# Weight conversions placed anew in a fused attention and two-MoE kernel: later ones apart, earlier ones at one step

## The chip, the cores and the metric

The kernel runs on one core of a Trainium2 chip. The metric is the device time in microseconds of one execution. Times below are of the kernel on its own, with all data in the chip's memory at the start.

## The reference

Three layers follow one another, all in float32 (the weights come in as float64 words and are used at a precision above one float32r product):

```python
kv  = einsum('bhsd,bhse->bhde', k, v)          # 8 batches, 8 heads, 576 tokens, 64 wide
x   = einsum('bhsd,bhde->bhse', q, kv)
x   = x / sqrt(mean(x*x, -1) + 1e-6) * g_norm  # then reshaped to 4608 tokens x 512
h   = x @ w_in;  x = relu(h)**2 @ w_out        # 512 -> 2048 -> 512, weights A
h   = x @ w_in;  out = (h * cos(h)) @ w_out    # 512 -> 2048 -> 512, weights B
```

## The kernel before

Every matrix product is made of three float32r products of a high and a low half (high x high, high x low, low x high), so each operand is split: ScalarE (ACT) casts the high half and VectorE (DVE) subtracts it to get the low one.

**Stage one** (`run_chunks`, L842) makes the attention, and with it one half of the first MoE layer (eight of the sixteen 128-wide slices of its hidden dimension). Its unit is a chunk: one tile of 512 tokens and one slice `f`. There are nine tiles; the last two (7 and 8) have 4 chunks each and the others 8, so `nA0` = 64 chunks. A chunk makes 12 matmuls into a bank (`layer_in`, L409), has relu and square (`act_relu2`), and two chunks later (`LAG`) 12 more (`layer_out`, L443). At a tile's last chunk `evict` (L424) copies the four accumulators out, the even ones on ACT, the odd ones on DVE, and stores each two of them to `p_d`. Up to chunk 49 (`nAtt`) the attention of later batches runs between the chunks.

**Stage two** (`run_slots`, L870) makes the rest by a scheme of seven products in place of eight for each 2x2 block product (Strassen's, in Winograd's form). A slot is one pair of token half-tiles and one group of hidden slices, with 84 first-product matmuls (L532, banks FA and FB) and the second products (L665, banks SA and SB) that follow 1.25 slots later (`LAG2`). There are 31 slots: 0 to 10 for the rest of the first MoE layer, 11 to 30 for the second. Slots 0 to 3 and 8 to 22 have matmuls of 512 columns, 4 to 7 and 23 to 30 of 384. In a slot DVE makes sums of hidden blocks, low halves (L642), differences (L618) and drains of the S banks (L693); ACT makes relu or the cosine's parts and the high halves (L641). Blocks of the inputs (`x_block`, L487 to L506) of a tile are made from about 0.64 slot before the tile's first slot to 0.5 after its start.

**The weight conversions** give stage two its weights: a raw block is loaded from memory, turned from float64 words to float32 (L121 to L135: four DVE steps, one ACT step, then one more DVE step), combined into seven blocks (four subtractions or additions, L199), split (cast L216 on ACT, L218 on DVE), and stored to `wi_d` (first weights) or `ws_d` (second), from where each slot loads them (L511, L516). `conv_steps` (L186) is a generator; its steps are placed at offsets 0, 0.25, 0.5, 0.75, 1.0, 1.25 chunks from the item's place in stage one and at 0, 0.07, 0.15, 0.22, 0.3, 0.4 slots in stage two (`Stream.place`, L728). The kinds of items:

- "seven" and "pair" (stage one): a half of a pair of slices, 512 elements a partition, for the second and the first weights; the load of the item after next is issued 1.4 chunks after an item's place, into the same two buffers.
- "pairs" (stage two): a whole pair, 1024 elements a partition, from float64: the heavy kind.
- "pairs32" and "sevens32" (stage two): a whole pair that stage one has already turned to float32 and stored in `wf_d`, so that only L199, L216 and L218 are left: the light kind.

The late stream has one raw buffer. An item's load is issued `lead` = 0.5 slot ahead of its place, but no earlier than 0.62 slot after the place of the item before.

What sets the order of the work is written by hand: all jobs have a position in chunks or slots, `run_jobs` emits them in that order between the matmuls, and the tile framework assigns buffers and semaphores and has some freedom in the order on an engine. All loads and stores of the parts named here are issued by the sync engine (SP), in order; POOL issues the attention's stores and the accumulating adds of the second MoE layer.

Of the kernel before, what the change touches and what calls it, by code (L numbers as in the profile page):

```python
# [22 lines left out]
def kernel(  # L23
# [15 lines left out]
    nc = tc.nc  # L39
# [3 lines left out]
    NH = NF // 2  # L43
    NP = NH // 2
# [14 lines left out]
    FS = [NH // 2 if any(TILES[u][0] <= t * TOK < TILES[u][0] + 2 * TILES[u][1] for u in SHORT) else NH for t in range(NTILE)]  # L59
# [364 lines left out]
    def evict(t, i, acc):  # L424
        if i % 2 == 0:
            evs[t, i // 2] = ev_p.tile([P, 2, 512], F32, tag="ev", name="ev")
        both = evs[t, i // 2]
        if i % 2 == 0:
            nc.scalar.copy(out=both[:, 0, :], in_=acc)
        else:  # L430
            nc.vector.tensor_copy(out=both[:, 1, :], in_=acc)  # L431
            nc.sync.dma_start(out=p_d[t][:, i - 1:i + 1, :], in_=both)

    def layer_out(t, f):
        wh, wl = (x[:, 1, :] for x in wts[0, f])
        gh, gl = gs.pop((t, f))
        for i in range(NKC):
            if f == 0:
                accs[i] = bank_tile(f"acc{i}")
            o = accs[i]  # L440
            cs = slice(i * P, (i + 1) * P)
            for n, (a, m) in enumerate(((wh, gh), (wh, gl), (wl, gh))):
                nc.tensor.matmul(  # L443
                    o, a[:, cs], m[:], start=(f == 0 and n == 0), stop=(f == FS[t] - 1 and n == 2), skip_group_check=True
                )
            if f == FS[t] - 1:
                evict(t, i, o)
# [258 lines left out]
    nA0 = len(chunks)  # L706
    nAtt = 49
# [6 lines left out]
    def pos(slot):  # L714
        return nA0 + slot + 0.002
# [27 lines left out]
    def pairs_in(m, ps, kind="pair"):  # L743
        return [(kind, m, p, i) for p in ps for i in range(2)]
# [5 lines left out]
        w_at += [n + step * k for k in range(len(new))]  # L750
    for new, n0, n1 in (
        (
            pairs_in(0, range(NP, 2 * NP), "seven") + pairs_in(1, range(2 * NP), "seven"),
            10,
            nAtt + 1,
        ),
        (pairs_in(0, range(NP, 2 * NP)), nAtt + 1, nA0 - 5),
    ):
        w_items += new
        w_at += [n0 + (n1 - n0) / len(new) * k for k in range(len(new))]  # L760
    w_stream = Stream(load_w, conv_w, w_items)
    w_stream.place(w_at, 0.5, range(2 * NH - NRAW, 2 * NH - NRAW + 2))
    late_stream = Stream(load_w, conv_w, (
        [("pairs", 1, p, 0) for p in range(NP)]
        + [(kind, 0, p, 0) for kind in ("pairs32", "sevens32") for p in range(NP // 2, NP)]
        + [("pairs", 1, p, 0) for p in range(NP, 2 * NP)]
    ))
    late_stream.place([pos(n) for n in (0.55, 1.25, 2.5, 3.2, 4.5, 5.2, 6.5, 7.2, 8.5, 9.3, 11.5, 12.3)], 0, lead=0.5)

    kv_stream = Stream(load_kv, kv_mm, [(b, c) for b in range(B) for c in range(NSC)])  # L770
    starts = [(-13, 1), (-3, 0.8)] + [(-3 + 7 * (b - 1), 7 / (2 * NKC)) for b in range(2, B)]
# [3 lines left out]
    for b, (s0, ds) in enumerate(starts):  # L775
        for i, u in enumerate(att_units(b)):
            n = s0 + i * ds
# [21 lines left out]
    for k, (m, t, q) in enumerate(slots):  # L799
# [7 lines left out]
        for f, i in enumerate(S_ORDER):  # L807
            at(pos(k + LAG2 + (f - 2.7) * PH), load_ws, k, i)
            n = LAG2 + (f - 1.6) * PH
# [14 lines left out]
        for b, f in BLOCKS.items():  # L824
            for a, fn in enumerate(chain):
                late = 0.3 if f == 7 and a > 1 else 0
                n = (f + late + 0.25 * (a + 1)) * PH
# [159 lines left out]
```

## Time and profile before

| | |
|---|---|
| median of 3 runs | 1575.92 us (1573.0 to 1578.34) |
| profiled execution | 1575.98 us, span 1574.1 us |
| granted TensorE clock, mean | 0.995 |
| PE busy | 98% of the span |
| DVE, ACT, POOL busy | 83%, 70%, 7% |
| DMA | 445.58 MB, mean 283 GB/s |
| stage one | 0 to 457 us |
| slots 0 to 10 | 457 to 874 us (with the last second products running on) |
| slots 11 to 30 | from about 874 us to the end |

The span runs from the first to the last instruction; 1.9 us of the execution lie outside it. PE is TensorE with its matmuls, PEld its weight loads, and a window's clock is the granted share of full speed: 1.00 is 2.4 GHz and 0.50 is 1.2 GHz, the engine's two levels. A row of waits names the engine that stood, the line of the instruction that stood, the instruction whose end released it, the sum, the count and the longest. SPq is SP's queue of DMA issues.

### The profile page before, as it was taken

Reading aid. Unit: us, or ns where it says so; the run is one execution under the profiler, and the core shown is the slowest. Engines: PE = TensorE matmul, PEld = TensorE weight load, DVE = VectorE, ACT = ScalarE, POOL = GpSimd, SP = SyncE. Lnnn points to the kernel's source line nnn. Section 1 sums busy time; section 2 is a strip of 40 time slices with the busy share of each in tenths; the row PEclk is TensorE's granted clock in tenths of the full one; section 3 lists DMA queues with packets and bytes.
Section 4 is the critical chain, followed back from the end, with each engine's and each line's share of the span. In section 5 each row is a group of like instructions: output and inputs, shape, how many; then the busy total and the mean of one; then the engine's idle time right before and its main releaser. Section 6 shows DMA issues by size and latency. Waiting matters only on the chain.

```text
span 1574.1 us, 24732 instructions
## 1 busy us (share of the span) xinstructions
PE 1535.6 (98%) x9080; PEld 1344.6 (85%) x9080; DVE 1309.8 (83%) x1747; ACT 1102.3 (70%) x1554; POOL 114.5 (7%) x181
## 2 busy tenths in 40 slices
PE   6899999999998999999999999999999999999998
PEld 4677777778787878998888899999999999999998
DVE  6987888887788999979889978967896788779777
ACT  6877777775566565656657777777777777777775
POOL 1122111110000000000000000000000000000001
PEclk9999999999999999999999999999999999999999
DMA  9858989777898898999997798787888788999896
GB/s 337 282 180 243 281 268 282 223 212 227 280 329 311 296 353 298 402 400 356 347 374 232 274 322 250 238 293 221 255 235 293 215 247 264 292 323 306 275 336 168
DMA packets 232072, 445.58 MB, mean 283 GB/s; under 512 B 19728, under 2 KB 144144, under 8 KB 231952
## 3 DMA queue, kind: packets, MB, share of 16 engines
q1 hardware_dynamic: 219536, 406.91, 74.7%
q0 software_dynamic: 12256, 37.10, 10.8%
q8 instruction: 72, 1.18, 0.3%
q14 instruction: 48, 0.39, 0.1%
q10 hardware_dynamic: 160, 0.00, 0.0%
HBM read 327.16 MB, written 91.23 MB: 266 GB/s over the span
## 4 chain that ended last, share of the span: by engine, by line
PE 74%; DMA 10%; DVE 9%; issue 3%; ACT 3%; SPq 0%; POOL 0%; DVEq 0%; ACTq 0%; POOLq 0%
PE SA L665 15%; PE SB L665 14%; PE FB L532 14%; PE FA L532 14%; PE acc L443 7%; PE l L409 6%; DMA wi_d<-raw 2%; DMA wi<-wi_d 1%; DMA raw<-in_wA 1%; DMA ws_d<-raw 1%; DMA raw<-in_wB 1%; DVE gl L642 1%; DVE sum L693 1%; DVE raw L218 1%; DMA xraw<-x_d 1%
## 5 line engine op out<-in xcount | busy, mean ns | idle before, releaser
L532 PE MATMUL FA<-xh,wi 128*128 128x512 f32 (+1 forms) x872 | 313.0, 371 | 1.0 <-ACT h L571 0.6
L532 PE MATMUL FB<-xh,wi 128*128 128x512 f32 (+1 forms) x864 | 311.7, 372 | 0.1
L665 PE MATMUL SA<-ws,gh 128*128 128x256 f32 x1008 | 232.9, 280 | 0.2 <-ACT part L690 0.2
L665 PE MATMUL SB<-ws,gh 128*128 128x256 f32 x1008 | 232.5, 280 | 0.0
L665 PEld LDWEIGHTS SB<-ws,gh 128*128 128x128 f32 x1008 | 183.3, 188 | 12.0
L665 PEld LDWEIGHTS SA<-ws,gh 128*128 128x128 f32 x1008 | 183.2, 188 | 12.1 <-ACT part L690 0.4
L532 PEld LDWEIGHTS FA<-xh,wi 128*128 128x128 f32 x872 | 163.5, 188 | 13.3 <-ACT h L571 1.0
L532 PEld LDWEIGHTS FB<-xh,wi 128*128 128x128 f32 x864 | 162.5, 189 | 11.5 <-ACT u L552 0.5
L665 PE MATMUL SA<-ws,gl 128*128 128x256 f32 x504 | 141.3, 280 | 0.3 <-DVE gl L642 0.3
L665 PE MATMUL SB<-ws,gl 128*128 128x256 f32 x504 | 141.3, 280 | 0.1
L642 DVE TENSOR_TENSOR gl<-y,gh 128x1024 fp32r<-128x1024 f32 (+1 forms) x98 | 109.5, 1117 | 35.7 <-ACT gh L641 35.5
L691 POOL DMA_DIRECT2D sum<-part x54 | 47.2, 874 | 1149.3 <-ACT part L690 561.6
L602 DVE SCALAR_TENSOR_TENSOR y<-y,h 128x1024 f32<-128x1024 f32 (+1 forms) x79 | 88.2, 1116 | 43.0 <-ACT y L598 42.8
L665 PE MATMUL SA<-gh,ws 128*128 128x512 f32 (+1 forms) x312 | 114.5, 379 | 6.6 <-ACT wh L216 4.2
L584 ACT ACTIVATE y<-h,zerob 128x1024 int32<-128x1024 f32 (+1 forms) x79 | 84.1, 1065 | 48.2 <-DVE h L558 48.1
L532 PE MATMUL FA<-xl,wi 128*128 128x512 f32 (+1 forms) x312 | 115.9, 371 | 0.0
L532 PE MATMUL FB<-xl,wi 128*128 128x512 f32 (+1 forms) x308 | 114.6, 372 | 0.0
L665 PE MATMUL SB<-gh,ws 128*128 128x512 f32 (+1 forms) x304 | 108.4, 370 | 0.0
L443 PE MATMUL acc<-gh,wh 128*128 128x512 f32 x256 | 100.6, 398 | 4.2 <-DVE ev L431 1.7
L693 DVE TENSOR_TENSOR sum<-SA,sum 128x1024 f32<-128x1024 f32 (+1 forms) x78 | 87.4, 1121 | 19.2 <-PE SA L665 14.9
L594 ACT ACTIVATE y<-y 128x1024 f32<-128x1024 f32 (+1 forms) x79 | 77.2, 977 | 34.7 <-DVE y L588 34.6
L443 PE MATMUL acc<-gl,wh 128*128 128x512 f32 x256 | 100.6, 393 | 0.3 <-DVE gl L421 0.3
(172 smaller groups left out, 3840.4 us busy)
## 6 DMA issues: line engine op xcount, KB each, us to landing
wi<-wi_d SPq DMA_DIRECT2D x217, 512.0 KB, 6.9
ws<-ws_d SPq DMA_DIRECT2D x217, 512.0 KB, 6.2
sum<-part POOLq DMA_DIRECT2D x33, 512.0 KB, 7.2
kvld<-in_kv SPq DMA_DIRECT2D x32, 512.0 KB, 7.6
ws_d<-raw SPq DMA_DIRECT2D x24, 448.0 KB, 4.5
q<-in_qT SPq DMA_DIRECT2D x32, 288.0 KB, 5.3
p_d<-ev SPq DMA_DIRECT2D x18, 512.0 KB, 4.9
wi_d<-raw SPq DMA_DIRECT2D x10, 896.0 KB, 7.1
```

The source lines that it names most:

```text
L218: nc.vector.tensor_tensor(out=l[:, lo:end], in0=a[:, lo:end], in1=as32(h), op=ALU.subtract)
L409: nc.tensor.matmul(ps, a[:, 0, cs], m[:], start=(c == 0 and k == 0), stop=(c == NKC - 1 and k == 2))
L443: nc.tensor.matmul(o, a[:, cs], m[:], start=(f == 0 and n == 0), stop=(f == FS[t] - 1 and n == 2), skip_group_check=True)
L532: nc.tensor.matmul(ps[:, pp, :], a, b, start=(n == 0 and (i in (0, 2) or i == 1 and not seeded(k))), stop=(n == 5), skip_group_check=True,)
L584: nc.scalar.activation(out=y.bitcast(I32), in_=hs[k, b], func=AF.Identity, bias=zerob)
L594: nc.scalar.activation(out=y, in_=y, func=AF.Sin, scale=math.pi)
L602: nc.vector.scalar_tensor_tensor(out=y, in0=y, scalar=-2.0 * math.pi, in1=hs.pop((k, b)), op0=ALU.add, op1=ALU.mult)
L642: nc.vector.tensor_tensor(out=l, in0=src, in1=as32(h), op=ALU.subtract)
L665: nc.tensor.matmul(ps[:, b, :], lhs, rhs, start=(n == 0 and (m == 0 or b % 2 == 0) and i in (0, 1, 2)), stop=(n == 5), skip_group_check=True,)
L691: nc.gpsimd.dma_start(out=e, in_=part, accum_op=ALU.add)
L693: nc.vector.tensor_tensor(out=e, in0=ps, in1=e, op=ALU.add)
```

## The change

Three edits. In `evict` the odd accumulators of the two short tiles (7 and 8) are copied by ACT too. In stage one, the conversions from chunk 10 on stand at one step up to `nA0 - 3` = 61: 34 items, 1.5 chunks apart, where 24 stood 1.667 apart from 10 to 50 and then 8 stood 1.125 apart to 59; their order mixes "seven" and "pair" items, and the two halves of pair 0 of the second layer's first weights are new among them. In stage two that pair is gone from the late list, which has 11 items at other places: pairs 1 (0.95), 2 (2.5), 3 (4.5), 4 (6.5), 5 (9.2), 6 (10.2), 7 (11.4) of the second layer are heavy, with the four light ones at 3.4, 5.4, 7.4 and 8.3. Before, heavy ones stood at 0.55, 1.25, 2.5, 3.2, 8.5, 9.3, 11.5 and 12.3 and the light ones at 4.5, 5.2, 6.5 and 7.2.

```diff
         both = evs[t, i // 2]
-        if i % 2 == 0:
-            nc.scalar.copy(out=both[:, 0, :], in_=acc)
+        if i % 2 == 0 or FS[t] < NH:
+            nc.scalar.copy(out=both[:, i % 2, :], in_=acc)
         else:
             nc.vector.tensor_copy(out=both[:, 1, :], in_=acc)
+        if i % 2:
             nc.sync.dma_start(out=p_d[t][:, i - 1:i + 1, :], in_=both)
...
     for new, n0, n1 in (
         (
-            pairs_in(0, range(NP, 2 * NP), "seven") + pairs_in(1, range(2 * NP), "seven"),
+            pairs_in(0, range(NP, 2 * NP), "seven")
+            + pairs_in(1, range(2), "seven")
+            + pairs_in(0, range(NP, NP + 2))
+            + pairs_in(1, range(2, 2 * NP), "seven")
+            + pairs_in(0, range(NP + 2, 2 * NP))
+            + pairs_in(1, range(1)),
             10,
-            nAtt + 1,
+            nA0 - 3,
         ),
-        (pairs_in(0, range(NP, 2 * NP)), nAtt + 1, nA0 - 5),
     ):
...
-    late_stream = Stream(load_w, conv_w, (
-        [("pairs", 1, p, 0) for p in range(NP)]
-        + [(kind, 0, p, 0) for kind in ("pairs32", "sevens32") for p in range(NP // 2, NP)]
-        + [("pairs", 1, p, 0) for p in range(NP, 2 * NP)]
-    ))
-    late_stream.place([pos(n) for n in (0.55, 1.25, 2.5, 3.2, 4.5, 5.2, 6.5, 7.2, 8.5, 9.3, 11.5, 12.3)], 0, lead=0.5)
+    late_stream = Stream(load_w, conv_w, [
+        ("pairs", 1, 1, 0), ("pairs", 1, 2, 0), ("pairs32", 0, 2, 0), ("pairs", 1, 3, 0), ("pairs32", 0, 3, 0),
+        ("pairs", 1, 4, 0), ("sevens32", 0, 2, 0), ("sevens32", 0, 3, 0),
+        ("pairs", 1, 5, 0), ("pairs", 1, 6, 0), ("pairs", 1, 7, 0),
+    ])
+    late_stream.place([pos(n) for n in (0.95, 2.5, 3.4, 4.5, 5.4, 6.5, 7.4, 8.3, 9.2, 10.2, 11.4)], 0, lead=0.5)
```

## Rows read from the trace of the kernel before

**Rows 1.** The page's busy time, share of the span and instructions.

```profile
PE 1535.6 (98%) x9080; PEld 1344.6 (85%) x9080; DVE 1309.8 (83%) x1747; ACT 1102.3 (70%) x1554; POOL 114.5 (7%) x181
```

**Rows 2.** Windows by stage: length, each engine's busy time, granted clock, DMA share, GB/s.

```profile
100.00:350.00 250.00, 248.69 (x1546) 194.08 (x1545) 206.07 (x471) 193.76 (x429) 46.16 (x86) 1.00 0.82 249
...
405.00:450.00 45.00, 41.91 (x182) 33.40 (x181) 35.85 (x65) 27.66 (x45) 0.00 (x0) 1.00 0.96 321
...
517.00:595.00 78.00, 76.88 (x338) 62.84 (x337) 73.37 (x74) 47.52 (x50) 0.00 (x0) 1.00 0.92 326
595.00:662.00 67.00, 67.00 (x348) 61.70 (x346) 60.62 (x67) 41.49 (x51) 0.00 (x0) 1.00 0.91 339
662.00:727.00 65.00, 61.18 (x336) 60.07 (x336) 52.64 (x62) 36.24 (x46) 0.00 (x0) 0.95 1.05 402
727.00:836.00 109.00, 108.90 (x501) 92.29 (x500) 95.05 (x97) 64.17 (x68) 0.00 (x0) 1.00 0.92 341
836.00:874.00 38.00, 38.00 (x169) 31.50 (x168) 37.08 (x37) 25.80 (x26) 0.00 (x0) 1.00 0.77 253
```

**Rows 3.** PE's waits in the whole span: us in total, times, longest.

```profile
PE SA L665 <- ACT wh L216: 4.2, 1, 4.2
PE SA L665 <- ACT gh L641: 2.3, 1, 2.3
...
PE acc L443 <- DVE ev L431: 1.7, 1, 1.7
```

**Rows 4.** Windows around the two largest waits of PE, columns as in rows 2.

```profile
492.00:498.00 6.00, 1.76 (x8) 1.21 (x7) 6.00 (x7) 2.58 (x4) 0.00 (x0) 0.86 0.80 326
498.00:504.00 6.00, 6.00 (x17) 4.66 (x17) 6.00 (x8) 4.03 (x5) 0.00 (x0) 0.57 0.93 329
704.00:711.00 7.00, 3.32 (x14) 2.49 (x13) 6.66 (x10) 3.71 (x5) 0.00 (x0) 0.78 1.05 401
711.00:716.00 5.00, 5.00 (x20) 5.00 (x20) 4.61 (x5) 2.82 (x4) 0.00 (x0) 0.62 1.05 413
```

**Rows 5.** Timeline at the first stall: start, duration, engine, line; idle before in brackets.

```profile
488.29 0.69 DVE L121 TENSOR_SCALAR e<-raw 128x1024 uint32<-128x1024 uint32 x1 [1.03 <-DMA raw<-in_wB]
...
495.18 1.22 DVE L135 SCALAR_TENSOR_TENSOR raw<-w,e 128x1024 f32<-128x1024 uint32 x1
496.32 1.22 DVE L693 TENSOR_TENSOR sum<-SA,sum 128x1024 f32<-128x1024 f32 x1
496.44 0.83 ACT L216 CAST wh<-raw 128x768 fp32r<-128x768 f32 x1 [3.42 <-DVE raw L135]
...
497.64 0.77 PE L665 MATMUL SA<-gh,ws 128*128 128x512 f32 x1 [4.24 <-ACT wh L216]
```

**Rows 6.** Timeline ahead of the second stall, ACT.

```profile
700.62 0.84 ACT L216 CAST wh<-raw 128x768 fp32r<-128x768 f32 x1 [5.40 <-DMA raw<-wf_d]
```

**Rows 7.** DVE's waits from 405 to 450 us.

```profile
DVE e L121 <- DMA raw<-in_wA: 7.2, 2, 3.9
```

**Rows 8.** SP's longest wait in 100:350; DMA issues: KB each, median us to landing.

```profile
SPq L145 <- DMA ws_d<-raw: 57.3, 21, 4.9
...
ws_d<-raw SPq DMA_DIRECT2D x24, 448.0 KB, 4.5
...
raw<-in_wA SPq DMA_DIRECT2D x24, 256.0 KB, 3.8
```

**Rows 9.** Conversion steps in slots 0 to 11, shapes apart: busy us, mean ns.

```profile
L199 DVE TENSOR_TENSOR raw<-raw 128x256 f32<-128x256 f32 x48 | 18.4, 420 | 0.3
L218 DVE TENSOR_TENSOR raw<-raw,wh 128x1024 fp32r<-128x1024 f32 x12 | 14.6, 1218 | 0.3 <-ACT wh L216 0.3
...
L126 DVE SCALAR_TENSOR_TENSOR w<-raw,w 128x1024 uint32<-128x1024 uint32 x8 | 9.7, 1217 | 0.0
```

**Rows 10.** Groups by line: copies of the accumulators on DVE and ACT.

```profile
L431 DVE COPY ev<-acc 128x512 f32<-128x512 f32 x18 | 12.3, 686 | 4.8 <-PE acc L443 4.8
...
L429 ACT COPY ev<-acc 128x512 f32<-128x512 f32 x18 | 10.3, 593 | 4.8 <-PE acc L443 4.8
```

## The prediction, made before the change was run

> **What bounds the kernel now.** I began with the busy shares of the page [rows 1]: TensorE is busy in 1535.6 of the 1574.1 us of the span, so about 38.5 us of idle time, and whatever it ran at half clock, is all that a change of order can win. The windows come next [rows 2], cut where the stages and slots end (a slot is 84 first-product matmuls, so its borders are counted from the matmuls). PE is idle 1.3 us in the attention part (100 to 350 us), 3.1 us at the end of stage one (405 to 450), 1.1 us in slots 2 and 3, nothing in 595 to 662, 3.8 us in 662 to 727, and next to nothing after. The rest lies ahead of 100 us, at the end, and in slot 1, and the change does not touch the first two.
>
> The waits of PE [rows 3] name the places: 4.2 us for the cast `wh` of a weight conversion, 2.3 us for a cast `gh`, 1.7 us for DVE's copy of an accumulator. Cut finer, both large waits show a second cost [rows 4]. From 492 to 498 PE was busy 1.76 of 6 us, so 4.24 idle; then for 6 us it was busy throughout at a granted clock of 0.57, which is mostly the 1.2 GHz level. That loses 6 x 0.43 = 2.6 us more, and with 0.2 at the edge the first stall cost **7.0 us**. The second: 7 - 3.32 = 3.7 us idle, 5 x 0.38 = 1.9 us in the row after it, and about 0.7 in matmuls at half clock before 711: **6.3 us**.
>
> Why the first happened stands in its timeline [rows 5]. The conversion of pair 1 (second in the late list, at 1.25) reached DVE at 488.29; its last step L135 ran at 495.18, and only behind it came the sum that empties bank SA, at 496.32. It ended at 497.5, and PE's next SA matmul began at 497.64. ACT's cast waited for the same L135. So DVE's queue was full, and the conversion stood ahead of a drain. The second has another cause [rows 6]: ACT stood 5.40 us at a cast because the raw weights of a light item had not landed, and everything behind it on ACT was late, the relu chain and `gh` among it. In the old list that item follows the one before by 0.7 slot, and its load is only issued 0.62 after that one's start, 0.08 slot ahead of its use: 2.4 us at 29 us a slot.
>
> **The change, part by part.** All sums are against the profiled execution, 1575.98 us, which is 0.06 above the median shown.
>
> *End of stage one.* Eight conversions stood 1.125 chunks apart there, which with a reload 1.4 chunks behind the use of two items earlier leaves 0.85 chunk, 4.6 us at 5.44 us a chunk. DVE waited 7.2 us, in two waits, for raw weights [rows 7], and the copy L431 behind them held PE for 1.7 [rows 3]. At 1.5 chunks the lead is 1.6 chunks, 8.7 us. A store and a load need about 4.5 + 3.8 us [rows 8], so most of it goes. The last two tiles' second and fourth copies (4 instructions, 0.69 us on DVE, 0.59 on ACT) [rows 10] leave that queue too; ACT has room (27.7 of 45 us), so I cost them at nothing; if ACT is late, a bank comes free 0.6 us late. Of 3.1 us idle I take **-2.6** (bounds -3.1 and 0). Two more conversions, halves of pair 0, stand at 58 and 59.5, and they take buffers of the block pool while the blocks of slot 0 are made; a late store there holds ACT, which the two chunks of lag (10.9 us) cover. The two halves issue 8 DMAs on SP where the whole issued 5, of equal bytes, beside loads not wanted before slot 0.
>
> *Attention part.* The step goes from 1.667 to 1.5 chunks, so some 26 items stand where there were 23. One costs DVE near 5 us (about 0.6 of a heavy late one, below), so 206 of 250 us busy becomes 219 [rows 2], and PE has 1.3 us idle to show for the present load. The reload lead falls from 1.93 to 1.6 chunks, 10.7 us at 6.7 us a chunk. SP already waits 57.3 us there, 21 times, for a store to land before a reload [rows 8]. Cover: that lead and the two chunks of lag. Bounds 0 and +8 (rival C). I take **+1.0**, near the present idle time. The Trainium skill ("DMA: Bandwidth & Descriptors", "Anatomy of one DMA") puts most of a DMA's fixed cost, about 2 us, into the receipt of its write, with a fit of 2.0 us plus bytes over 436 GB/s; worked out from the page, an estimate, store and load would take 5.7 us and this term would be 0. The trace has 8.3 us for the pair, and the measurement decides.
>
> *Slots 0 and 1.* Pair 0 is gone from 0.55 and pair 1 moves from 1.25 to 0.95, so DVE has one heavy item fewer and the other off its drains. A heavy item costs DVE 2 x 0.69 (L121, L123) + 3 x 1.22 (L126, L132, L135) + 4 x 0.38 (L199) + 1.22 and about 0.95 for its piece of three quarters (L218) = 8.7 us; a light one lacks the first five, and costs 3.7 [rows 5, 9]. The stall goes: **-7.0**. In its place: the item now stands just ahead of the first operand of the second products, wanted at 1.25, 0.3 slot or 5.7 us after it. One L121, an ACT step of about 1.1, two 1.22s, then the casts and the rest of that operand (0.8 + 1.0 + 1.2) come to 7.4 us, 1.7 late. I take **+2.0**; it is 0 if DVE starts early, and 5 if the wait costs half clock as the second stall did.
>
> *Slots 2 and 3.* One heavy item becomes light; the 1.1 us idle goes: **-0.8** (0 to -1.1).
>
> *Slot 7.* The item now has 0.28 slot, 8 us, from load to use in place of 2.4. The raw weights landed 5.40 us after ACT wanted them, so 5.7 us more lead just covers it. The stall goes: **-6.3** (0 if DMA, at 1.05 of its share there [rows 2], takes longer).
>
> *Slots 4 to 7, DVE.* Two light items become heavy (4.5 and 6.5), +2 x 5.0 us. DVE was busy 60.6 + 52.6 of 132 us, idle 18.8 [rows 2], with 6 of that in the stall. It fits on the sum, to 123 of about 126, but locally it is full. A drain may be late by one block of 12 matmul pairs (4.2 us at 384 columns) before PE feels it. Bounds: 0, and all 10; I take **+2.0**.
>
> *Slots 8 to 12.* The heavy item at 12.3 moves to 10.2, ahead of slot 11, whose window (836 to 874) has DVE busy 37.1 of 38 us while PE loses nothing; 727 to 836 has 14 us of room [rows 2]. Bounds 0 and 8; **+1.0**.
>
> Sum: -2.6 + 1.0 - 7.0 + 2.0 - 0.8 - 6.3 + 2.0 + 1.0 = -10.7, so 1575.98 - 10.7 = **1565.3 us**. With the best bounds all round it is -17.5, 1558.5.
>
> **Rivals.**
> A: the new waits (2 + 2 + 1 + 1 = 6 us) each drop the clock. Both stalls shown cost about 1.7 times their idle time [rows 4], so +4.2: 1569.5. Against it: the wait of 1.7 us at 418 left the clock at 1.00 in its window [rows 2, 3]. The Trainium skill ("TensorE: Matmul & The Clock Gate", "HAM oscillation") says that repeated waits re-throttle the engine and the return is paid each time; the trace agrees for the two large waits, not for the short one. By that rule this rival is the forecast.
> B: the stalls only move. The 0.95 item delays the first second product by as much as the 1.25 item did the drain, and DVE in slots 4 to 7 makes one stall of 6.3 us: -2.6 + 1.0 - 0.8 - 6.3 + 6.3 + 1.0 = -1.4, 1574.6. For it: the scheduler orders DVE's queue by its own idea of time, and moved no drain ahead of L135 [rows 5].
> C: reloads late in the attention part, five times, at what each of the two waits in rows 7 cost PE (3.1 / 2 = 1.55): +8 for +1, 1572.3. Against: 3.8 + 4.5 us is below the lead.
> D, slower: DVE becomes the bound from slot 4 on, and its idle time can't be used, as it is waiting for ACT and PE. Then all added DVE time is paid: +10 in slots 4 to 7 and +8 before slot 12 instead of +3, and each stretch drops the clock once, 2 x 2.6 more: -10.7 + 15 + 5.2 = +9.5, 1585.5. It turns the sign when over 13.7 of these 23.2 us are paid, and can be told from no change from 18.4 on. For it: slot 11 is already full. Against it: 595 to 662 ran DVE at 60.6 of 67 with no PE idle, so lateness is absorbed.
>
> **How the numbers follow.** About 0.3% (4.7 us) is what a measurement of this kernel can tell from no change, so faster means below 1571.2 and slower above 1580.6. Forecast 0.54, A 0.12: both faster, 0.66. B 0.17 and C 0.05: the same, 0.22. D: 0.12. The likeliest case alone spans 1558.5 (all new waits nil) to 1571. Leaving out D's upper part and a little at the bottom, the range is 1558 to 1577, which takes in A, B and C.
>
> **What would show it.** Right: no PE wait over 2 us between 457 and 914, the granted clock 1.00 in every 25 us there, no wait of DVE for raw weights behind chunk 50, PE idle near 1 us in 100 to 350. Wrong: a PE wait at the first second product with the clock at half behind it (B), PE waiting for drains around 4.5 to 5 or 6.5 to 7 or at slot 11 with DVE busy 99% (D), or many DVE waits for raw weights in the attention part (C). The forecast fails above all if DVE at 98% in slots 4 to 7 leaves PE no slack.

## The result and the profile after

The changed kernel takes **1584.59 us** (median of 5 runs, 1582.74 to 1585.82) against 1574.78 us for the kernel before in the same series: ratio **1.0058, interval [1.0043, 1.0074]**. It is slower by 0.6%, where the prediction had 1565.3 and 1558 to 1577. The profiled execution has a span of 1583.8 us, at a mean granted clock of 0.993.

Counted from the matmuls, slot 0 starts at 476.8 us, before at 457.2: stage one lost **19.6 us**. From the start of slot 0 to the start of slot 12 it is 406.6 us against 416.6: those slots won **10.0 us**. The other 19 slots moved by under 1 us. (By the same count slots 0 to 10 of the kernel before end at 836 us and slot 11 at 874; where the table of before and two of the expectations say slots 0 to 10, they mean 0 to 11.)

The busy row of the page, to be held against [rows 1], shows next to no change:

```profile
PE 1536.8 (97%) x9080; PEld 1345.3 (85%) x9080; DVE 1307.6 (83%) x1755; ACT 1103.2 (70%) x1562; POOL 114.0 (7%) x181
```

The windows by stage have the columns of [rows 2]; in the order of the rows: the attention part, the largest stall in it and the stretch behind, the end of stage one (moved by the 19 us), slots 0 and 1, 2 and 3, 4 to 7, 8 to 11.

```profile
100.00:350.00 250.00, 235.49 (x1457) 182.04 (x1456) 200.11 (x462) 181.98 (x404) 41.40 (x79) 0.97 0.82 248
175.00:182.00 7.00, 1.34 (x7) 0.81 (x5) 2.60 (x6) 0.73 (x2) 0.00 (x0) 0.73 0.96 243
182.00:188.00 6.00, 6.00 (x25) 4.33 (x26) 4.58 (x13) 3.57 (x8) 2.11 (x4) 0.74 0.73 195
424.00:469.00 45.00, 42.04 (x174) 34.23 (x173) 33.98 (x58) 25.82 (x41) 0.00 (x0) 0.92 0.97 316
476.00:530.00 54.00, 54.00 (x240) 44.72 (x239) 44.90 (x43) 38.56 (x41) 0.00 (x0) 1.00 0.92 322
530.00:606.00 76.00, 76.00 (x338) 62.94 (x337) 69.44 (x70) 46.21 (x49) 0.00 (x0) 1.00 0.89 309
606.00:735.00 129.00, 124.86 (x678) 118.79 (x677) 118.47 (x135) 76.87 (x95) 0.00 (x0) 1.00 0.97 357
735.00:885.00 150.00, 149.06 (x675) 124.59 (x674) 136.94 (x139) 93.27 (x97) 0.00 (x0) 1.00 0.92 340
```

PE is idle 14.5 us in 100 to 350, where it was 1.3 [rows 2], and DVE is *less* busy there, 200 against 206 us, although the change asks it for more: fewer items passed in that time. At the end of stage one the idle time is as large as before (3.0 against 3.1), now with the clock down to 0.92 behind it. In slots 0 to 3 it is nil.

PE's longest waits by now, whole span (columns as in [rows 3]; the last line is from before); both `SA` waits of before are gone:

```profile
PE ss L346 <- DVE m L359: 12.7, 6, 5.7
PE o L285 <- DMA kvld<-in_kv: 11.0, 5, 8.6
PE l L409 <- ACT r L418: 3.1, 4, 1.1
PE acc L444 <- ACT ev L429: 3.0, 1, 3.0
...
PE ss L346 <- DVE m L359: 1.3, 2, 0.7
```

The second row lies ahead of 100 us and is as before. The first is new in size, 12.7 us against 1.3: the attention's norm has a single bank, `ss`, which DVE's step L359 empties. What DVE waits for in 100 to 350 says why it is late: 19.1 us in 9 waits for raw weights, where the same view of before (the last two lines) adds up to 5.4 in 3.

```profile
DVE e L121 <- DMA raw<-in_wA: 11.7, 5, 5.6
...
DVE e L121 <- DMA raw<-in_wB: 7.4, 4, 2.8
...
DVE e L121 <- DMA raw<-in_wB: 3.9, 2, 3.5
...
DVE e L121 <- DMA raw<-in_wA: 1.5, 1, 1.5
```

One stall in full, from the timelines of SP, DVE and PE (start, duration, engine, line):

```profile
165.56 0.68 SPq L221 DMA_DIRECT2D ws_d<-raw  x1
166.34 2.51 SPq L273 DMA_DIRECT2D kvld<-in_kv  x2
173.03 1.28 SPq L145 DMA_DIRECT2D raw<-in_wA  x3
...
179.36 0.43 DVE L121 TENSOR_SCALAR e<-raw 128x512 uint32<-128x512 uint32 x1 [5.63 <-DMA raw<-in_wA]
181.37 0.45 DVE L359 SCALAR_TENSOR_TENSOR m<-ss,r 128x288 f32<-128x288 f32 x1
...
181.87 0.61 PE L346 MATMUL ss<-sh,ones 128*128 128x288 f32 x1 [5.66 <-DVE m L359]
```

A conversion's last store is issued at 165.56, among the loads of keys and values. SP then stands until it has landed, since the reload goes into the same buffer, and issues the reload at 173.03. DVE gets at it at 179.36 and had waited 5.63 us; the norm's step L359 stands behind it in DVE's queue, and PE behind that. From 175 to 188 us the granted clock is also down, to 0.73 and 0.74 in the two windows above.

### The profile page after: what moved, and what is told of

Read it like the earlier page. It is cut to its first block, busy times and chain, and to the rows that moved or that the text cites. A ratio compares the mean times of both kernels' runs of the same rounds, so it can differ in the third digit from the quotient of the medians.

```text
span 1583.8 us, 24760 instructions
## 1 busy us (share of the span) xinstructions
PE 1536.8 (97%) x9080; PEld 1345.3 (85%) x9080; DVE 1307.6 (83%) x1755; ACT 1103.2 (70%) x1562; POOL 114.0 (7%) x181
## 3 DMA queue, kind: packets, MB, share of 16 engines
q0 software_dynamic: 12256, 37.10, 10.7%
## 4 chain that ended last, share of the span: by engine, by line
PE 70%; DMA 13%; DVE 6%; issue 6%; ACT 4%; SPq 1%; POOL 0%; DVEq 0%; POOLq 0%; ACTq 0%
PE FB L533 14%; PE FA L533 14%; PE SA L666 14%; PE SB L666 14%; PE acc L444 6%; PE l L409 5%; DMA ws_d<-raw 3%; DMA sum<-part 2%; DMA ws<-ws_d 2%; DMA raw<-in_wA 1%; DMA wi_d<-raw 1%; DVE raw L218 1%; DVE gl L643 1%; DMA kvld<-in_kv 1%; DVE sum L694 1%
## 5 line engine op out<-in xcount | busy, mean ns | idle before, releaser
L666 PEld LDWEIGHTS SA<-ws,gh 128*128 128x128 f32 x1008 | 183.2, 188 | 12.5 <-ACT part L691 0.7
L533 PEld LDWEIGHTS FA<-xh,wi 128*128 128x128 f32 x872 | 163.2, 188 | 10.7
L666 PE MATMUL SA<-gh,ws 128*128 128x512 f32 (+1 forms) x312 | 110.5, 371 | 0.5 <-issue 0.3
L444 PE MATMUL acc<-gh,wl 128*128 128x512 f32 x256 | 102.0, 398 | 0.0
```

The source lines that it names most:

```text
L444: nc.tensor.matmul(o, a[:, cs], m[:], start=(f == 0 and n == 0), stop=(f == FS[t] - 1 and n == 2), skip_group_check=True)
L533: nc.tensor.matmul(ps[:, pp, :], a, b, start=(n == 0 and (i in (0, 2) or i == 1 and not seeded(k))), stop=(n == 5), skip_group_check=True,)
L666: nc.tensor.matmul(ps[:, b, :], lhs, rhs, start=(n == 0 and (m == 0 or b % 2 == 0) and i in (0, 1, 2)), stop=(n == 5), skip_group_check=True,)
```

## The experiments

Five theories stand against each other, and the expectations use these letters. **T**: the reload is placed too late. **L**: DVE has too much work. **S**: SP, an in-order queue, stands for a store to land, and other transfers are late behind it. **E**: the DMA engines are full in the bursts of five loads of keys and values (one batch's, issued together every 7 chunks). **K**: the cycle of the two raw buffers is too slow for the step of 1.5 chunks; three of the expectations have it under an earlier name, T2. (O, in two of them, blames the new order of the items.) "Before" and "after" are the two kernels of the case, and each ratio is to before in the run's own series.

### Which part of the change wins and which loses

Late places alone, on the kernel before:

```diff
-        [("pairs", 1, p, 0) for p in range(NP)]
...
+        ("pairs", 1, 1, 0), ("pairs", 1, 2, 0), ("pairs32", 0, 2, 0), ("pairs", 1, 3, 0), ("pairs32", 0, 3, 0),
+        ("pairs", 1, 0, 0), ("sevens32", 0, 2, 0), ("sevens32", 0, 3, 0),
...
+    late_stream.place([pos(n) for n in (0.95, 2.5, 3.4, 4.5, 5.4, 6.5, 7.4, 8.3, 9.2, 10.2, 11.4, 12.3)], 0, lead=0.5)
```

> The late list alone: the kernel before, with the new places for the late conversions and pair 0 kept among them (at 6.5, so the heavy ones after it move one place on and the last stands at 12.3). If the two parts are independent (stage one lost about 19 us, the slots won about 9), stage one ends as before, slot 0 begins at 457 us, slots 0 to 10 take 408 to 411 us in place of 417.5, and the time is 1565 to 1569 us. If the slots won only because pair 0 had left them, slots 0 to 10 take 415 to 420 and the time is 1572 to 1578.

Measured 1569.14 us, 0.9962 [0.9951, 0.9974]; slots 0 to 11 take 406.7 us. The other way round, after's stage one with the old late places (without pair 0):

> Stage one and the copies as changed, the late conversions at their old places (without pair 0). If the parts are independent, slot 0 begins at 475 to 478 us, the stall in slot 7 (6.3 us) comes back and the one in slot 1 partly; slots 0 to 10 take 410 to 417 us and the time is 1586 to 1594 us. If the loss in stage one came with the late list, slot 0 begins at 457 to 460.

1589.27 us, 1.0092 [1.0076, 1.0109]. The late part wins about 6 us alone and the rest loses about 14; together that is the loss of the whole change to within 1 us. In slots 0 to 11 the two overlap: they take 408.9 us without pair 0 at the old places, 406.7 with it at the new ones, and 406.6 with both edits. Slot 0 starts at 478.6 us in this run, so the fault lies in stage one.

There the change has three parts: a new order, a new step, and copies on ACT. The new order at the old step up to chunk 50, and the rest behind it:

```diff
-            nA0 - 3,
-        ),
...
+    w_at += [10 + (nAtt - 9) / 24 * k for k in range(24)] + [nAtt + 1 + (nA0 - nAtt - 4) / 10 * k for k in range(10)]
```

> The changed kernel with the old step of 1.667 chunks up to chunk 50 (24 items) and the other 10 items at 1.1 up to 61. Theory T (the reload of the raw buffers comes late at the closer step, and DVE stands on it) and theory L (DVE has too much to do at the closer step) both expect PE idle of 1 to 3 us in 100 to 350 us, slot 0 at 459 to 464 us and a time of 1567 to 1572 us. Theory O (the new order, which puts pair items among the seven items) expects that the attention part still loses 10 us or more: slot 0 at 468 or later, time over 1576 us.

1581.31 us, 1.0043 [1.0028, 1.0058]. The attention part was whole again, and the loss went to where the step was now 1.1 chunks. Its windows:

```profile
100.00:350.00 250.00, 249.38 (x1549) 194.63 (x1549) 206.87 (x472) 193.85 (x429) 46.15 (x86) 1.00 0.82 248
440.00:460.00 20.00, 13.01 (x46) 9.18 (x46) 16.24 (x29) 12.03 (x20) 0.00 (x0) 0.89 1.00 316
```

In the attention part the order is innocent and the step makes the loss. At the end of stage one this run has two more items than before besides the shorter step, and does not tell the two apart. The copies, back on DVE in the kernel after:

```diff
-        if i % 2 == 0 or FS[t] < NH:
+        if i % 2 == 0:
```

> The changed kernel with the two short tiles' second and fourth copies on DVE again. The stall at 435 us (3.0 us, at half clock after) names an accumulator copy on ACT. If the moved copies cause it, it shrinks by 2 us or more and the time is 1577 to 1582 us; if ACT and DVE are late for another reason (raw weights late for an item at the end of stage one), the stall stays with DVE's copy named and the time is 1583 to 1587 us.

1587.95 us, 1.0075 [1.0059, 1.0091], against 1.0058 for after: the copies on ACT do no harm and may help a little. The stall at the end of stage one is 1.9 us here against 3.0, at a clock of 1.00, and still names a copy on ACT (L429); slot 0 starts at 476.9 as in after. Added to the late places alone:

> The kernel before with the new late places and the copies of the last two tiles on ACT (stage one's conversions as before). Both theories: the late places alone gave 1569.1 us; the copies take DVE's copy out of the chain that held PE for 1.7 us at the end of stage one, so 1566.5 to 1569.5 us, slot 0 at 456 to 459 us. If the copies cost something on ACT, 1570 to 1573 us.

1568.03 us, 0.9947 [0.9935, 0.9959], slot 0 at 457.2: as expected, and better than both kernels.

### Why the step of 1.5 chunks loses

The place of the reload inside an item (theories T and S): 1.73 chunks behind an item's place in the attention part, in before and in after; the conversion's last steps 0.33 chunk later in before; all steps closer and the reload at 1.0 in after.

```diff
-                    steps = (0, 0.25, 0.5, 0.75, 1.0, 1.25, 1.4)
+                    steps = (0, 0.25, 0.5, 0.75, 1.0, 1.25, 1.73 if n < nAtt else 1.4)
...
+                    steps = (0, 0.25, 0.5, 0.75, 1.33, 1.58, 1.73) if n < nAtt else (0, 0.25, 0.5, 0.75, 1.0, 1.25, 1.4)
...
+                    steps = (0, 0.2, 0.4, 0.6, 0.8, 0.95, 1.0)
```

> The kernel before with one number changed: in the attention part the reload of a raw buffer is issued 1.73 chunks behind an item's place in place of 1.4, so its lead is 1.6 chunks as in the changed kernel, at the old step, order and load. Theory T expects DVE waits for raw weights of 10 us or more in 100 to 350 us, PE idle of 8 us or more there, slot 0 at 467 to 478 us and a time of 1584 to 1596 us. Theories L and O expect no change: slot 0 at 457 us, time 1573 to 1578 us.

> The changed kernel with the reload of a raw buffer issued 1.73 chunks behind an item's place in the attention part in place of 1.4, so that the store it waits for has mostly landed and SP does not stand. Theory S (SP's queue is full at the closer step: it stands at every reload until the store has landed, each burst of five key and value loads puts it further back, and it does not catch up before the next): reloads go out less than 13 us behind PE's position after a burst, where they were 19, PE idle under 7 us in 100 to 350 us, slot 0 at 458 to 467 us, time 1565 to 1575 us. Theory T (what counts is the lead of the load): slot 0 at 476 us or later, time 1584 us or more.

> The kernel before, with the last two steps and the reload of a conversion 0.33 chunk later in the attention part (1.33, 1.58, 1.73), so that from the last store to the next use there are 1.75 chunks as in the changed kernel, at the old step, order and load of DVE. Theory T2: DVE waits of 8 us or more for raw weights and PE idle of 6 us or more in 100 to 350 us, slot 0 at 465 us or later, time 1582 us or more. Theory L: as before, slot 0 at 456 to 459 us, time 1573 to 1579 us.

> The changed kernel, with the steps of a stage-one conversion closer together (at 0, 0.2, 0.4, 0.6, 0.8, 0.95 chunks, reload at 1.0), so that from an item's last store to the next use of its buffer there are 2.05 chunks in place of 1.75 (2.08 in the kernel before). Theory T2 (the cycle of the two raw buffers, convert, store, land, load, no longer fits in two items at the closer step): DVE waits for raw weights under 6 us and PE idle under 4 us in 100 to 350 us, slot 0 at 458 to 464 us, time 1565 to 1572 us. Theory L (DVE has too much to do at the closer step): slot 0 at 472 us or later, time 1580 us or more.

The late reload in before: 1577.44 us, 1.0014 [1.0003, 1.0025]. In after: 1577.95, 1.0017 [1.0008, 1.0026], some 6 us *better* than after itself, with slot 0 at 467.0. Longer conversions in before: 1576.56, 1.0004 [0.9994, 1.0013]. Shorter ones in after: 1584.13, 1.0054 [1.0036, 1.0072]. T falls: of the 21 items that start between 110 and 345 us, at least 20 had their reload issued within 0.5 us of the landing of the store ahead of it, in before, in after and in all four of these runs, wherever it was placed. In after, SP issues a reload 5 to 19 us after PE is at its place. S explains little: SP's waits for a store ahead of a reload, in 100 to 350, fell only from 61.8 to 59.5 us with the later reload, so why that helps in after stays open. None of the four wins the loss back. The two runs with moved steps changed less than their edits say: from its first step to the issue of its last store an item takes 10.6 us on average with the closer steps, as in after, and 9.6 us with the later ones, where before has 9.7. So they hardly touch the cycle, and their times speak neither for L nor against T2.

Less work for DVE (L), with two of its steps left out of stage one's conversions:

```diff
-        nc.vector.scalar_tensor_tensor(
-            out=w, in0=low, scalar=28, in1=w, op0=ALU.logical_shift_right, op1=ALU.bitwise_or
-        )
...
-        nc.vector.scalar_tensor_tensor(
-            out=e, in0=raw[..., 1], scalar=0x80000000, in1=e, op0=ALU.bitwise_and, op1=ALU.bitwise_or
```

> The changed kernel with two of the seven steps by which DVE turns a stage-one item's float64 words into float32 left out (the low bits and the sign), 1.4 us of about 5 per item, so that DVE has less to do per chunk than in the kernel before. Theory L: PE idle under 4 us in 100 to 350 us, slot 0 at 457 to 463 us, time 1564 to 1571 us. Theory T2: the stores come a little earlier, but land and reload as late; DVE still waits 8 us or more for raw weights, PE idle 7 us or more, slot 0 at 466 us or later, time 1574 us or more.

1582.72 us, 1.0043 [1.0027, 1.0059]. The window of the attention part:

```profile
100.00:350.00 250.00, 236.54 (x1454) 181.31 (x1453) 174.72 (x418) 180.81 (x403) 41.67 (x79) 0.98 0.80 246
```

and what DVE waited for in it:

```profile
DVE e L121 <- DMA raw<-in_wA: 17.6, 7, 5.6
DVE e L121 <- DMA raw<-in_wB: 13.8, 6, 5.8
```

DVE is busy 25 us less than in after, PE still idle 13.5, and DVE's waits for raw weights rose from 19.1 to 31.4. About half of the work freed became waiting for raw weights, and each of the four things that T2 expected came (slot 0 at 476.2 us). L falls.

The loads of keys and values issued by POOL instead of SP (S against E), in after and in the version with the late places alone:

```diff
-        nc.sync.dma_start(out=t[:n], in_=kv[r0:r0 + n])
+        (nc.gpsimd if b > 1 else nc.sync).dma_start(out=t[:n], in_=kv[r0:r0 + n])
```

> The changed kernel with the key and value loads of batches 2 to 7 issued by POOL in place of SP (POOL is busy 7% of the span). Theory S: SP loses its bursts, DVE waits for raw weights under 8 us and PE idle under 5 us in 100 to 350 us, slot 0 at 457 to 465 us, time 1563 to 1573 us. Rival E (the DMA engines themselves are too full in a burst, so a store or load lands late whoever issues it): slot 0 at 472 us or later, time 1579 us or more.

> The kernel before with the new late places (as in the run of the late list alone, 1569.1 us) and the key and value loads of batches 2 to 7 issued by POOL. Theory S: the attention part has next to no PE idle at the old step, so nothing is won there: 1567 to 1570 us; a loss would mean that POOL's queue holds the attention's stores back.

1592.5 us, 1.0109 [1.0094, 1.0124], and 1574.74, 0.9993 [0.9977, 1.0009]: worse in both, by 8 and 5 us. SP's longest wait for a store rose from 5.4 us (first line, after) to 10.2 (second line, after with the loads on POOL):

```profile
SPq L145 <- DMA ws_d<-raw: 43.6, 14, 5.4
...
SPq L145 <- DMA ws_d<-raw: 58.5, 14, 10.2
```

So S by the issuing queue falls: with the burst gone from it, SP waits more. The mean time that the last store of an item takes to land hardly moved (from 5.4 to 5.3 us in after, from 5.0 to 5.2 in the other); the longest landing of a raw load did, from 5.5 to 9.2 and from 5.0 to 8.6 us. This fits E, but does not show it: POOL also stood 15 and 17 us, from 100 to 365, for a free buffer of keys and values, ahead of the attention's stores in its queue, and no run parts the two.

### The cycle of two buffers

Theory K came from DVE's and SP's timelines. For the 21 items of after that start between 110 and 345 us, the first step L121 is on average 10.6 us ahead of the issue of the last store (L221), the reload follows 5.4 us later, and its use 6.0 us after that: **22.0 us** from one use of a buffer to the next, an item per 11.0 us from two buffers. (The expectation of the third buffer splits the same sum as 7.2, 5.0 and 9.9.) Asked for was 1.5 chunks of 6.7 us, 10.0. The sum alone proves nothing, since two buffers in turn make it twice the pace in any kernel: before has 22.3, and its step asks for 1.667 x 6.7 = 11.2. What differs is the slack between the landing of the reload and its use. Without it an item needs 19.5 us in before (9.7 + 4.9 + 4.9 for the landing; single items up to 25.5), against 22.3 us in two steps: 2.7 us of slack, and 3 of 21 items used within 0.3 us of landing. Against the 20.0 us of two steps of 1.5 chunks the same 19.5 leaves 0.5; in after, 11 of 21 items are used within 0.3 us of landing. With a third buffer, an item per 7.3 us would do by the sum of 22.0, an estimate. Its memory comes from the attention's outputs, and a control takes that memory alone. A third run spreads the loads of keys and values.

```diff
-        xo = att_p.tile([P, HS], F32, tag="xo", name="xo", bufs=6)
+        xo = att_p.tile([P, HS], F32, tag="xo", name="xo", bufs=4)
...
-        ev_p, pools["raw"] = right("ev", 2), right("conv", 2)
+        ev_p, pools["raw"] = right("ev", 2), right("conv", 3)
...
-    kv_stream.place([s0 - 0.5 for s0, _ in starts for c in range(NSC)], 0)
+    for b, (s0, _) in enumerate(starts):
+        for c in range(NSC):
+            at(s0 - 0.5, kv_mm, b, c)
+            at(s0 - 0.5 + (1.2 * c if b > 0 else 0), kv_stream.advance)
```

The first two edits are the third buffer (with one more load ahead), the first alone is the control, the third alone the spread (on the kernel after, all of them).

> The kernel after with a third buffer for raw weights in stage one (its memory taken from the attention's outputs, six buffers to four). Theory K (the two buffers' cycle): one item holds its buffer for about 22 us (7.2 us of conversion, 5.0 until the reload is issued, 9.9 until it is used, in the kernel after), so two buffers give one item per 11.2 us, the pace measured in every run so far, and the change asks for 10.0 us. Three buffers would give one per 7.4 us: DVE's waits for raw weights in 100 to 350 us fall from 19.1 to under 5 us, PE's idle time there from 14.5 to under 4 us, slot 0 starts at 457 to 464 us instead of 476.8, and the whole takes 1564 to 1571 us. Rival E (the DMA engines are full in the bursts of the attention's loads, and land late whatever the buffers): PE's idle time stays above 10 us, slot 0 starts at 472 or later, 1579 to 1586 us.

> Control for the third buffer: the kernel after with four buffers for the attention's outputs instead of six, and two raw buffers as they are. Theories K and E: as the kernel after, slot 0 at 474 to 480 us, 1582 to 1587 us. If it comes out below 1578 us or above 1590 us, the outputs' buffers matter by themselves and the run with the third buffer must be read against this one.

> The kernel after with the five loads of keys and values of a batch issued 1.2 chunks apart instead of together. Theory K: the mean landing stays about as it is, the pace stays near 11 us per item, slot 0 at 472 to 478 us, 1579 to 1586 us, with the stalls no longer behind the bursts but all over the stretch. Rival E: without the burst the landings are short, SP's wait for a store in 100 to 350 falls from 43.6 to below 25 us, slot 0 starts at 460 to 466 us, 1567 to 1574 us.

Third buffer 1573.26 us, 0.9984 [0.9972, 0.9996]; control 1587.11, 1.0069 [1.0055, 1.0082]; spread 1581.83, 1.0038 [1.0026, 1.0051]. One buffer took 13.8 us off its control, without any change in work or order. DVE's waits for raw weights in 100 to 350, 19.0 us in the control, are gone altogether, and slot 0 starts at 463.1 against the control's 481.0. The time itself lies 2 us above what K expected, and PE is still idle 8.2 us:

```profile
100.00:350.00 250.00, 241.80 (x1490) 187.97 (x1490) 206.64 (x478) 187.50 (x415) 42.63 (x80) 0.99 0.83 253
```

Slots 0 to 11 take 411.0 us in that run, 4.4 more than in after: PE waits 2.2 us for DVE's step L563 in slot 0, and the granted clock from 470 to 490 us is 0.91. What ACT and DVE wait for in 100 to 350 is new; neither before nor after has one such row:

```profile
ACT wh L216 <- DMA ws_d<-wh: 3.7, 2, 2.6
ACT r L418 <- DMA ws_d<-wh: 2.6, 1, 2.6
ACT g L419 <- DMA ws_d<-wh: 2.2, 2, 1.8
DVE e L121 <- DMA wi_d<-wh: 2.0, 1, 2.0
```

The high halves of a conversion (`wh`) lie in the eight temporary buffers that relu's `r` and `g` take too, until their store has landed. With the raw buffers no longer short, these are next, though not alone: ACT's waits for the attention's output read back (L259, `xraw` from `x_d`) are 12.5 us in that stretch, against 8.8 in the control and 6.0 in after. The spread alone came out in K's interval (1579 to 1586), and its slot 0 at 468.5 between the two theories' intervals; the longest landing of an item's last store fell from 11.2 to 6.9 us, the mean from 5.4 to 4.8, and SP's wait ahead of a reload did not fall (44.9 us against 43.6): the bursts lengthen the cycle, but they are not its bound. Both edits together:

> The kernel after with both: a third buffer for raw weights and the loads of keys and values 1.2 chunks apart. With the third buffer alone DVE no longer waited for raw weights in 100 to 350 us, but ACT and DVE waited 10.8 us for stores of the high halves to land (wh, whose 8 temporary buffers are the ones that relu uses), a wait that neither before nor after has, and slot 0 started at 463.1 us, 5.9 behind before. Theory K2 (after the raw buffers the temporary buffers are the next to be short, held by slow stores): the spread loads shorten the landings, those waits fall below 5 us, slot 0 starts at 457 to 461 us, 1566 to 1571 us. Rival D2 (the rest is DVE's load, 207 of 250 us): the waits for wh change little in effect, slot 0 stays at 462 to 465 us, 1572 to 1576 us.

1564.85 us, 0.9931 [0.9919, 0.9944], slot 0 at 454.1, 3 us earlier than in before. The attention part:

```profile
100.00:350.00 250.00, 249.60 (x1547) 194.49 (x1546) 216.06 (x500) 197.69 (x437) 45.98 (x86) 1.00 0.84 262
```

PE is idle 0.4 us there while DVE is busy 216 us, more than in any window above. The waits for stores of the high halves are down from 10.8 to 1.9 us, so K2's sign came, and its time was too careful; but ACT's waits for the attention's output fell too, from 12.5 to 6.2, so K2 is not shown to be the only cause of the rest. D2 falls, and L with it for good. Last, the third buffer at the old step, with late places and copies:

> The kernel before with the new late places, the copies on ACT (1568.0 us) and a third buffer for raw weights. Theory K: at the old step of 1.667 chunks the two buffers just keep up in the attention part (4.8 us of DVE's waits for raw weights in 100 to 350), so nothing is gained there; at its end, where the step is 1.125 chunks and DVE waits 10.2 us for raw weights behind 350 us, the third buffer takes them to under 3 us and PE's idle time in 412 to 457 from 3.0 to under 1 us: 1564.5 to 1567.5 us. Rival: the shortage moves to the temporary buffers, as in the run with the denser step, and it is 1568 to 1572 us.

**1563.31 us, 0.9925 [0.9911, 0.9939]**, the best of the study, though its interval overlaps that of the run above. From 350 to 460 us DVE's waits for raw weights are down from 10.2 us (late places and copies) to 5.5, PE's idle time in 412 to 457 from 3.0 to 1.8, neither as far as expected (3 and 1); what is left are two waits for DVE's step L260. Slot 0 starts at 453.2, 4.0 us before the run without the buffer. So the cycle cost time at the end of stage one in the kernel before as well. SP's wait in 100 to 350 stayed as large as in before [rows 8], although the slack there is now 13 us:

```profile
SPq L145 <- DMA ws_d<-raw: 58.5, 20, 5.4
```

## Why the prediction was wrong

**Slots 0 to 11: right in sum.** The terms there add up to -9.1, and -10.0 was measured; the late places alone gave -9.9. That the sum is so close is in part luck, since misses of either sign cancel. By stretch, with borders counted from the matmuls: slots 0 and 1 -7.8 for -5.0, since the +2.0 for a late first operand (whose terms add up to 7.2 us, not 7.4) did not come; 2 and 3 -1.8 for -0.8; 4 to 7 -2.4 for -4.3, as new short stalls of up to 1.6 us stand there; 8 to 11 +2.0 for +1.0. The mechanisms of the rivals A, B and D did not show in these slots: the clock is 1.00 in all their windows above, with those short waits in them, as it was beside the wait of 1.7 us in before; PE is not idle at all in slots 0 to 3; and DVE at 118.5 of 129 us in slots 4 to 7 went with 4.1 us of PE idle.

**Attention part: the step that failed.** "I take +1.0", with the cover "that lead and the two chunks of lag", bounds 0 and +8. At chunk 49 after was 17.8 us behind before (383.8 against 365.9), so the term measured +17.8, and the third buffer with the spread loads brings it to 366.5, at the same step of 1.5 chunks and in the same order. Three things were wrong in that step.
First, the lead of 10.7 us was counted from the reload's *place*, and held against two median landings of 4.5 and 3.8 us [rows 8]. But the reload was only issued when the store had landed, and the store not before the conversion ended. The sum to check was what an item needs of its buffer, conversion and both landings, 9.7 + 4.9 + 4.9 us in before, against two steps of 10.0: that leaves 0.5 us, and single items take up to 25.5. The 57.3 us that SP stood, 21 times [rows 8], already said that every reload there left as soon as it could, and so that its place set nothing.
Second, the two chunks of lag cover the first MoE layer's products, not the attention. Its norm goes through one bank, emptied by DVE in queue order behind a conversion that waits.
Third, the bound of +8 priced five waits at 1.55 us each. There were nine, of up to 5.6 us, and after the longest the clock fell as well. Rival C was the right mechanism at less than half its size, and was given a chance of 0.05.

The page's rule weighed there (the Trainium skill, "DMA: Bandwidth & Descriptors", "Anatomy of one DMA") would have put the term at 0, further off still; the page gives its fit for DMAs issued by GpSimd, and these are issued by SP. The trace of after has, in 100 to 350, medians of 5.1 us for the 448 KB store and 3.5 us for the 256 KB load, and 13.8 us from the issue of the store at 165.56 to the use at 179.36.

**End of stage one: wrong by its own means.** "-2.6" was to come from a wider step; from chunk 49 to slot 0 after took 93.1 us against 91.3, so 1.7 us more. The wait on DVE's copy L431 did go, but PE's idle time stayed at 3.0 us: a 3.0 us wait on ACT's copy L429 took its place at 435. In ACT's queue that copy stood behind a conversion's cast L216, which had waited 2.35 us for DVE, and a block's cast L506; two conversions were bunched on DVE there, the second after a wait of 2.60 us for raw weights. The term itself could be had: the third buffer at the old step brought slot 0 to 453.2, 4.0 us ahead of before.

**What would have shown it** was named rightly: many waits of DVE for raw weights in the attention part (C), and PE idle time there far from 1 us. Both came.

## What to carry to other kernels

Before a stream is made denser, add up what one item needs of its buffer: from first use to last store, that store's landing, the reload's landing. Leave out the slack between landing and next use, and look at the longest items as well as the mean. Divide by the number of buffers; a step near or below that was paid here by the bound engine, whatever work was saved elsewhere. A queue that stands for a store ahead of every reload is no sign of a full cycle: SP did so in before, with 2.7 us of slack, and with the third buffer at the old step, with 13. When one buffer is added, look in the waits for the next pool that is held by the same stores. A lag covers only the work that goes through it, so check for every consumer in the same engine's queue how many banks it has.

## What was not expected of the hardware

Moving a burst of loads from SP's queue to POOL's did not shorten what SP waits for a store (10.2 us at the longest against 5.4), and cost 5 to 8 us in two kernels. The Trainium skill ("DMA: Bandwidth & Descriptors", "Issuing engines are not separate DMA queues") says that transfers run on the same 16 DMA engines and interleave, whichever engine starts them; the trace agrees in that the longest landing of SP's raw loads grew, from 5.5 to 9.2 us, when POOL issued the burst, and here issuing them all from SP was the better choice. The section "Queues, rings and completion order" of that page of the Trainium skill adds that a completion is written only after every earlier write of that DMA engine, across its queues; no run here tells this from mere sharing of the engines.

An engine at 86% of its time need not bound anything: DVE was busy 216 of 250 us with PE idle for 0.4, and 200 of 250 with PE idle for 14.5.
